# A searched instruction order replaced by another, with GpSimd as a second engine for two of VectorE's steps

## The chip, the cores and the metric

The kernel runs on one core of a Trainium2 chip. The core has five engines that work side by side, each with its own queue that is served strictly in order: TensorE (PE; weight loads and matmuls), VectorE (DVE), ScalarE (ACT; exponentials and tanh), GpSimd (POOL) and SyncE (SP), which here only issues DMA transfers. Engines wait for each other through semaphores. The metric is the device time of one execution in microseconds.

## The reference, cut to what matters

The input x has 2048 tokens of 640 channels in bfloat16. There are 32 heads of 20 channels, and the tokens are cut into 4 segments of 512. All weights are bfloat16.

```
h   = x + A(layernorm(x));   out = h + silu(layernorm(h) @ w1) @ w2        # w1: 640 x 1728

A:  q, k, v = x @ wq, x @ wk, x @ wv          # per head, per segment of 512 tokens
    for each segment:
        p     = softmax(q @ k.T * scale + causal mask)
        a_mem = (phi(q) @ M) / (phi(q) @ z + 1e-6)      # phi(t) = t + 1 if t > 0 else exp(t)
        o     = g * a_mem + (1 - g) * (p @ v)           # g = sigmoid(beta), per head
        M    += phi(k).T @ v ;  z += sum(phi(k))        # memory for the segments that follow
    return concat(o) @ wo
```

## The kernel before, in words

Work is declared as tasks, each with its engine (or the engines that may take it), what it reads and what it writes. In which order the tasks are issued, on which engine, and in which buffer slot, is written out by hand in one list, ORDER: an entry `qe030x/D:0` means task qe030x on VectorE with slot 0 of the pool that it allocates; /A is ScalarE, /G GpSimd, no letter the first engine that the task names. A tracker turns the list into one queue for each engine, with a semaphore wait wherever a task needs what another engine wrote. The list came from a search outside the kernel, over estimated durations; the kernel holds only its outcome. Nothing is reordered when it runs: a task that waits holds up all that stands behind it on its engine.

The tasks, by the first letters of their names:

- `x`, `w_`: loads of tokens and weights. `n1_st`, `n1_r`, `n1_ap`: statistics of the first layer norm (VectorE, L719 and L722), the power -0.5 of the variance (GpSimd, L735; its addition of eps on GpSimd, L732, or on VectorE, L729), the apply (VectorE, L741). `n2_` is the second layer norm, with the same lines.
- For segment 0 the normalized block of 128 tokens is transposed by TensorE (`n1_tp`, L750) and copied out of PSUM in one piece (`n1_te`, L759 on ScalarE, L760 on VectorE); for the others, and for n2, by a DMA transpose (`n1_tr`, `n2_tr`, L765).
- `pr`: q and k projections, five chunks each (L826); `qe` copies them out of PSUM (L834 ScalarE, L835 VectorE). In segment 0 each is done in two halves of two blocks, x and y. `v`, `ve`: the same for v (L793, L803, L804). The 12 columns of q and k that don't fit the first five chunks are gathered by small DMAs (`vt`) into a tile that is zeroed beforehand (`vz`, L847: one on VectorE, the one of segment 0 on GpSimd). In segment 0 q, k and the gathered tile lie in the memory of w2, which is loaded later.
- `re_wq`, `re_wk`: the weights of q and k put into chunk order by copies (L683 ScalarE, L685 VectorE).
- `qk`: scores of four heads at once (L912); `e`: their exponentials into a PT buffer of seven (ScalarE, L923); `mk`: the causal mask on the diagonal blocks (GpSimd, L934); `av`: the product with v (L955); `oe`: its evacuation (L968, L970); `tn`, `nm`, `ad`: turning back to tokens, division and adding (L984, L988; L1001 to L1021; GpSimd L1029).
- `ex`, `pha`, `phb`: phi(q) and phi(k), as the exponential (ScalarE, L866), max(t, 0) + 1 (VectorE, L873) and the minimum of the two (VectorE, L878). `kt`, `mz`, `ma`, `mb`: the memory, with a DMA transpose (L1072), products (L1077), sum and mask.
- `ot`, `wo`, `rs`: DMA transpose of the attention's output (L1116), output projection (L1124), residual (L1132). `h1`, `th`, `s`: first layer of the MLP (L1159, its short last tile L1153), tanh (L1168) and silu (L1174). `h2`, `o`, `out`: second layer (L1201), residual (L1214), store (L1219).
- `warm`: a tanh over a zero tile that fills the unused rows of w2 (L588), first on ScalarE. `fill`: matmuls on zeros, issued where TensorE has nothing to do (L607).

Segments overlap: projections of the next one, and the MLP of the one before, stand between the scores of this one.

Of the kernel before, what the change touches and what calls it, by code (L numbers as in the profile page):

```python
# [5 lines left out]
ACT = mybir.ActivationFunctionType  # L6
# [318 lines left out]
D = 640  # L325
# [31 lines left out]
qe000x:0 re_wk3 pr011x:1 qe020x:0 n1_tp2:2 x8:4,5,6,10 qe010x:0 n1_tp3:6 qe030x/D:0 re_wk4/A pr021x:4 qe011x n1_te2  # L357
qe001x/D pr041x:5 beta qe021x/D x4:7,8,9,11 n1_te3/D w_w1_0:0 n1_st9:1 w_w1_2 qk0x0:0 lsc0 qe041x:0 e0x0:0 e0x2
pr040x:4 pr031x:5 w_wv:0 n1_st7:3 pr041y:6 vz0/G:0 qk1x0:0 n1_r7 qe040x qe041y e1x2:1 lsc1 pr030y:7 pr040y:4 pr031y:6
qe031x/D e1x0 qe040y mk0x_0 w_w1_4 qe031y qk2x0:0 n1_st6:2 e2x2:2 qe030y/D pr011y:5 n1_st4:4 e2x0 pr001y:4 pr000y:7  # L360
n1_r4/D mk1x_0 qk3x0:0 mk2x_0 pr021y:6 qe000y/D qe021y/D vpad1 pr010y:7 n1_st5:6 qe001y/D mk2x_256 e3x2:3 e3x0 qe011y
n1_ap7:0 pr020y:2 vt04 vt08 v00:0 mk1x_256 qe020y vt01 qe010y ex011:0 ex031:1 vpad0 lsc2 qk4x0:2 ve00/D:0 vt011 e4x0:6
n1_r6/D pha011:0 vt05 n1_st8:5 v01:6 mk0x_256 vt02 e4x2 qk0yb0:0 vt06 mta0 ve01/D zf0 phb011 v03:4 pha001:1 mk3x_0
vt03 vt00 n1_r5/D lsc3 pha031:2 ex001:2 mtb0 e0yb0:4 e0yb2 n1_ap4:1 vt07 vt09 n1_ap6:2 av0x:6 av2x:7 n1_r9/D mk4x_0
vt010 n1_ap5:3 qk1yb0:0 ve03 mk3x_256 phb031 v02:4 e1yb2:5 oe0x/D:0 e1yb0 oe2x/D:1 mk4x_256 qk7x0:0 ve02/D e7x2:0 e7x0
n1_tr4:0 tn0x:6 mm1 mm6 n1_tr5 av1x:7 kt01:0 oe1x/D:0 n1_tr6 qk5x0:2 w_w1_3 tn1x:7 av3x:0 e5x0:2 nm0x:0,0 nm1x:1 e5x2
oe3x/D:0 mk7x_0 mk7x_256 tn2x:6 fill3:1 qk6x0:0 av4x:7 av7x:4 e6x2:1 nm2x:2 v11:5 pha051:0 e6x0 oe7x/D:1 phb001 ve11:1
mk0yb_0 n1_tr7 mk6x_0 mk6x_256 tn7x:3 v10:0 mk5x_0 ex051:0 ex021:1 oe4x/D:1 qk0ya0:4 mk5x_256 e0ya0:3 tn3x:2 mk0yb_256
zf1 nm7x:0 kt00:1 e0ya2 av6x:3 w_w2_4 ve10/D av5x:0 oe6x/D:0 nm3x:3 tn6x:1 oe5x/D:0 mk1yb_0 nm6x:1 fill2:3 qk1ya0:2
tn5x:0 tn4x:6 nm5x:2 av0y:7 pr100:1 e1ya2:1 nm4x:0 oe0y:1 e1ya0 w_wo:0 n1_st11:7 qk2yb0:4 ot1:0 mz00:0 mz01 phb051 ot0  # L370
mm7 mk1yb_256 e2yb0:6 ma00:0 v12:2 pha021:1 qe100/D:0 ve12/D e2yb2 qk2ya0:4 ex071:2 phb021 e2ya0:0 wo1:0 e2ya2
qk3ya0:2 rs1 n2_st1:0 e3ya0:2 mk2yb_0 wo0:6 n2_r1/D kt02:1 e3ya2 mk2yb_256 mm0 qk4ya0:0 rs0 e4ya0:3 kt03:0 n2_st0:4
v13:4 e4ya2 mz02:6 ve13/D av2y:7 qk3yb0:0 ex041:1 n2_r0 pha041:1 oe2y/D:0 mz03 pr141:4 e3yb2:4 n2_ap1:3 e3yb0 av1y:5
qk4yb0:0 phb041 ma01/A:1 n2_ap0:1 qe141/D:0 w_w1_1 tn0y:7 mk3yb_0 oe1y/D:1 ex061:0 kt05:1 nm0y:3 n2_tr1:0 e4yb2:6
e4yb0 n2_tr0 pr121:6 qk5ya0:2 tn2y:7 qe121/D:0 epsg1 nm2y:0 tn1y:0 e5ya2:0 pr101:1 e5ya0 qk5yb0:4 nm1y:1 pha141:2
# [901 lines left out]
```

## Time and profile before

| what | us |
|---|---|
| median of 3 runs (302.84 to 304.95) | 302.98 |
| the profiled execution | 302.65 |
| its span, first to last instruction | 300.9 |
| TensorE matmuls busy | 288.7 (96%) |
| VectorE busy | 234.4 (78%) |
| ScalarE busy | 230.5 (77%) |
| GpSimd busy | 135.8 (45%) |

The span is what the profile shows from the first instruction to the last; the execution's own time has 1.75 us around it. Matmuls are pipelined, so a busy TensorE isn't always one at its peak. In the views, "waits" give who waited for whom, in total, how often and the longest; the chain is followed back from the last instruction to what released it; a group's row has the line, the engine, the operation, its output and input, the count, then busy time, mean duration in ns, and idle time before it.

### The profile page before, as it was taken

The numbers are of one execution on the slowest core, as the hardware profiler recorded it, in microseconds if no ns is written. First come the engines' busy times: TensorE is split into PE (matmuls) and PEld (weight loads), VectorE is DVE, ScalarE is ACT, GpSimd is POOL, SyncE is SP. The second block draws the span as 40 slices with busy tenths as digits, with TensorE's granted clock in tenths as the row PEclk, the third lists the DMA queues.
The fourth block names the chain that finished last, engine by engine and source line by source line (L and its number), as shares of the span: only waits on it lengthen the run. The fifth ranks groups of instructions, "written<-read, shape, count | busy, mean of one in ns | idle before, by whom it ended". The sixth has DMA issues, their size and how long they took to land.

```text
span 300.9 us, 7531 instructions
## 1 busy us (share of the span) xinstructions
PE 288.7 (96%) x2994; PEld 169.5 (56%) x2994; DVE 234.4 (78%) x553; ACT 230.5 (77%) x337; POOL 135.8 (45%) x246
## 2 busy tenths in 40 slices
PE   8899888999999999989999899999999999999996
PEld 6675545555555455666643445556564457764575
DVE  6989887878798979879899976967868687835523
ACT  3889898999999999989889979998999741004500
POOL 2537843544566664445746715465395640200000
DMA  7953595556535320253662330233161004130002
GB/s 259 332 183 61 122 202 121 124 144 116 96 72 103 74 59 1 37 119 63 99 164 47 35 68 2 45 70 59 20 89 46 0 2 109 38 96 24 22 22 89
DMA packets 53603, 25.85 MB, mean 86 GB/s; under 512 B 44032, under 2 KB 52480, under 8 KB 53568
## 3 DMA queue, kind: packets, MB, share of 16 engines
q1 hardware_dynamic: 52144, 23.81, 36.5%
q10 hardware_dynamic: 1424, 1.56, 1.5%
q8 instruction: 24, 0.39, 0.6%
q14 instruction: 11, 0.09, 0.1%
HBM read 10.41 MB, written 2.62 MB: 43 GB/s over the span
## 4 chain that ended last, share of the span: by engine, by line
PE 66%; ACT 13%; DVE 12%; DMA 5%; issue 2%; POOL 1%
PE ps_all L1201 18%; PE ps_all L1159 15%; PE ps_all L826 10%; ACT PT L923 9%; PE ps_all L1124 7%; PE ps_all L912 6%; PE ps_all L955 5%; PE ps_all L793 3%; DMA oT<-otok 3%; DVE xn_rot L741 2%; DVE stt L719 2%; DVE oTs L970 1%; DMA xT<-xn_rot 1%; ACT th L1168 1%; ACT ex L866 1%
## 5 line engine op out<-in xcount | busy, mean ns | idle before, releaser
L923 ACT ACTIVATE PT<-ps_all 128x1024 bf16<-128x1024 f32 (+1 forms) x168 | 156.8, 987 | 10.0 <-PE ps_all L912 9.1
L934 POOL TENSOR_SCALAR_AFFINE_SELECT PT<-PT 128x512 bf16<-128x512 bf16 x128 | 80.8, 651 | 55.7 <-ACT PT L923 54.8
L1201 PE MATMUL ps_all<-w_sb,sT 128*128 128x320 bf16 (+2 forms) x462 | 65.5, 295 | 0.0
L1159 PE MATMUL ps_all<-hT,w_sb 128*128 128x512 bf16 (+1 forms) x325 | 63.3, 337 | 0.4 <-DVE otok L1003 0.2
L1168 ACT ACTIVATE th<-ps_all 128x512 f32<-128x512 f32 (+1 forms) x70 | 34.1, 509 | 34.6 <-PE ps_all L1159 27.0
L1201 PEld LDWEIGHTS ps_all<-w_sb,sT 128*128 128x128 bf16 x462 | 43.1, 98 | 19.0 <-issue 1.9
L1174 DVE SCALAR_TENSOR_TENSOR sT<-th,ps_all 128x512 bf16<-128x512 f32 (+2 forms) x70 | 38.0, 560 | 16.9 <-ACT th L1168 16.4
L1159 PEld LDWEIGHTS ps_all<-hT,w_sb 128*128 128x128 bf16 x325 | 29.3, 98 | 24.1 <-issue 3.2
L735 POOL TENSOR_TENSOR rst<-rst,eps_c 128x1 f32<-128x1 f32 x32 | 19.9, 623 | 23.7 <-DVE rst L729 22.3
L719 DVE BATCH_NORM_STATS2 stt<-x_tok 128x6 f32<-128x320 bf16 x64 | 27.9, 477 | 0.8 <-DMA x_tok<-in_A_x_dram 0.6
L1029 POOL TENSOR_TENSOR otok<-on 128x320 bf16<-128x320 bf16 x24 | 19.0, 797 | 17.8 <-DVE on L1021 17.8
L1124 PE MATMUL ps_all<-wo_sb,oT 128*128 128x320 bf16 x160 | 24.1, 300 | 1.9 <-DMA oT<-otok 1.6
L1214 DVE SCALAR_TENSOR_TENSOR x_tok<-ps_all,x_tok 128x640 bf16<-128x640 f32 (+3 forms) x18 | 13.3, 745 | 14.1 <-PE ps_all L1201 13.8
L955 PE MATMUL ps_all<-PT,Vx 128*32 128x256 bf16 (+3 forms) x576 | 23.7, 287 | 0.5 <-ACT PT L923 0.2
L970 DVE TENSOR_SCALAR oTs<-ps_all,lsc 128x512 bf16<-128x512 f32 (+1 forms) x33 | 20.3, 622 | 1.8 <-PE ps_all L955 1.1
L1021 DVE TENSOR_TENSOR on<-ps_all,rd 128x640 bf16<-128x640 f32 x24 | 19.8, 824 | 0.8
L1124 PEld LDWEIGHTS ps_all<-wo_sb,oT 128*128 128x128 bf16 x160 | 14.7, 98 | 9.7 <-issue 2.4
L741 DVE TENSOR_SCALAR xn_rot<-x_tok,mvt,rst 128x640 bf16<-128x640 bf16 x32 | 18.1, 572 | 2.2 <-POOL rst L735 2.1
L793 PE MATMUL ps_all<-wv_sb,xT 128*128 128x320 bf16 x120 | 18.2, 300 | 1.3 <-DMA xT<-xn_rot 1.0
L826 PE MATMUL ps_all<-xT,wqr 128*128 128x512 bf16 x75 | 18.7, 380 | 0.6 <-issue 0.6
L826 PE MATMUL ps_all<-xT,wkr 128*128 128x512 bf16 x75 | 18.7, 380 | 0.3 <-ACT PT L923 0.3
L1132 DVE TENSOR_TENSOR x_tok<-ps_all,x_tok 128x640 bf16<-128x640 f32 x16 | 13.1, 818 | 7.1 <-PE ps_all L1124 7.0
(90 smaller groups left out, 364.2 us busy)
## 6 DMA issues: line engine op xcount, KB each, us to landing
w_sb<-in_B_w_dram SPq DMA_DIRECT2D x5, 432.0 KB, 10.1
x_tok<-in_A_x_dram SPq DMA_DIRECT2D x3, 640.0 KB, 8.6
w_sb<-in_B_w_dram SPq DMA_DIRECT2D x3, 480.0 KB, 4.7
out_dram<-x_tok SPq DMA_DIRECT2D x9, 160.0 KB, 1.9
out_dram<-x_tok ACTq DMA_DIRECT2D x6, 160.0 KB, 1.8
QKV<-QK SPq DMA_DIRECT2D x12, 72.0 KB
sT<-in_A_wq_dram SPq DMA_DIRECT2D x1, 800.0 KB, 5.8
sT<-in_A_wk_dram SPq DMA_DIRECT2D x1, 800.0 KB, 7.4
```

The costliest lines, as they stand in the source:

```text
L719: T.add(DV, lambda e, hh=hh: e.bn_stats(out=stt[:, s, 6 * hh:6 * hh + 6], in_=xb[:, 320 * hh:320 * hh + 320]), reads=R((xa, xsub)), writes ...
L741: T.add(eng, lambda e: e.tensor_scalar(out=xn_rot[:, xn.slot, :], in0=x_tok[:, b % 12, :], scalar1=mvt[:, s, 0:1], scalar2=rst[:, s, :], o ...
L793: fns.append(lambda e, c=c, hh=hh: e.matmul(bank(ps, hh)[:, 0:320], lhsT=xT_[:, c, 128 * i:128 * i + 128], rhs=wv_sb[:, c, 320 * hh:320 * ...
L826: fns = [lambda e, kc=kc: e.matmul(bank(ps)[:, lo:hi], lhsT=wt[:, kc, c, :], rhs=xT_[:, kc, lo:hi], start=(kc == 0), stop=(kc == NC - 1)) ...
L923: T.add(AC, lambda e: e.activation(out=pt[:, pta.slot, q0:q0 + 2, 0:width], in_=sc3[:, b0:b0 + 2, 0:width], func=ACT.Exp, scale=SCALE), re ...
L934: T.add(PO, lambda e: e.affine_select(out=v, in_=v, pattern=[[0, 4], [1, 128]], compare_op=ALU.is_ge, fill=0.0, base=0, channel_multiplier ...
L955: fns.append(lambda e, j=j, r=r, h=h, pa=pa, pt=pt, co=co, q0=q0, ji=ji: e.matmul(bank(po)[32 * r:32 * r + 32, q0:hi], lhsT=Vx[:, vx.slot, ...
L1124: fns.append(lambda e, c=c, hh=hh: e.matmul(bank(ps, hh)[:, 0:320], lhsT=oT[:, c, 128 * i:128 * i + 128], rhs=wo_sb[:, c, 320 * hh:320 * h ...
L1159: fns = [lambda e, c=c: e.matmul(bank(ps)[:, lo:hi], lhsT=w1_sb[:, c, 128 * f:128 * f + 128], rhs=hT[:, c, lo:hi], start=(c == 0), stop=(c ...
L1168: T.add(AC, lambda e: e.activation(out=th[:, tha.slot, lo:hi], in_=bank(ps)[:, lo:hi], func=ACT.Tanh, scale=0.5), reads=R((ps, [0])), writ ...
L1174: T.add(DV, lambda e: e.scalar_tensor_tensor(out=sT[:, f, lo:hi], in0=th[:, tha.slot, lo:hi], scalar=1.0, in1=bank(ps)[:, lo:hi], op0=ALU. ...
L1201: fns.append(lambda e, f=f, t0=t0, fr=fr, hh=hh, n=n: e.matmul(bank(pa, hh)[:, 0:n], lhsT=sT[:, f, t0:t0 + 128], rhs=w2_sb[:, fr, c0 + 320 ...
```

## The change

The list ORDER is a new one, found by the same kind of search with all DMA transposes taken as late. Beside it some tasks change their form or get another engine to choose from:

- a max/add of phi (`pha`) and a norm apply (`ap`) may run on GpSimd; in the list 27 of 48 `pha` and 11 of 32 `ap` do (4 of the first norm, 7 of the second);
- the gathered tile is zeroed on VectorE only (`vz0` and `vz1`);
- q of segment 0 is projected and copied in three pieces, of block 0 (u), block 1 (v) and blocks 2 and 3 (y), where it was two halves;
- the evacuation of a segment-0 transpose is two instructions, of three and of two chunks, which may run on different engines; readers of it wait for both;
- there are eight PT buffers for seven.

The warm-up `warm` stands no longer first on ScalarE but among the exponentials of segment 0. TensorE's order keeps almost all of its sequence behind 90 us; the projections of segments 0 and 1 and the tail are reordered most. The core of the diff (of the list, its beginning):

```diff
-WH = [(0, 0), (0, 1), (1, 0), (1, 1)]
+WH = [(0, 0), (0, 2), (0, 1), (1, 0), (1, 2), (1, 1)]
+def XS(b0, b1):
+    return [10 * k + b for b in range(b0, b1) for k in range(2)]
...
 ORDER = """
-epsc:0 zpad x0:0 iota sel halfc x1:1 w_q:0 vz1:0 n1_st0:5 x2:2,3 n1_st1:3 n1_r0 n1_r1/D warm:0 n1_ap0:0 n1_ap1:1
-fill29:7 n1_tp0:0 n1_te0:0 re_wq2:0 re_wq3 n1_st2:7 fill3:2 n1_tp1:2 w_k n1_r2 n1_te1 n1_st3:0 re_wq0/A fill8:4
-pr020x:4 re_wq1/A re_wk0:0 pr030x:5 re_wq4 re_wk1/A mt0 n1_ap2:2 pr000x:6 re_wk2 pr010x:7 n1_r3 n1_ap3:3 pr001x:0
+iota:0 zpad x0:0 halfc vz0:0 sel epsc x1:1 n1_st1:0 n1_r1 w_q:0 n1_st0:1 n1_ap1:0 x2:2,3 n1_r0/D w_k beta re_wq1:0
+fill25:7 n1_tp1:0 n1_st3:2 n1_te1a:0 n1_ap0/G:1 fill11:2 n1_tp0:2 re_wq3 re_wq4 n1_r3 n1_te1b re_wq0/A pr010v:4
+n1_ap3/G:2 n1_te0b/D pr000v:6 pr030v:0 re_wq2/A n1_te0a qe000v:0 pr020v:5 pr040v:7 pr000u:1 qe010v:0 n1_st2:3
...
-        "PT": 7, "oTs": 2, "on": 2, "rd": 4, "otok": 1, "oT": 1,
+        "PT": 8, "oTs": 2, "on": 2, "rd": 4, "otok": 1, "oT": 1,
...
-        G.task(f"{tag}ap{b}", {DV: 0.46}, e_apply, ...)
+        G.task(f"{tag}ap{b}", {DV: 0.46, PO: 0.78}, e_apply, ...)
...
-                src = ps_all[:, 512 * ps.slot:512 * ps.slot + 640].rearrange("p (c t) -> p c t", c=NC)
-                o = dst[:, :, 128 * i:128 * i + 128]
+            for k, (c0, c1) in enumerate(((0, 3), (3, NC))):
+                    src = ps_all[:, 512 * ps.slot + 128 * c0:512 * ps.slot + 128 * c1].rearrange("p (c t) -> p c t", t=128)
+                    o = dst[:, c0:c1, 128 * i:128 * i + 128]
...
-                for hh, (b0, b1) in enumerate([(0, 2), (2, 4)] if s == 0 and (c, w) in SPLIT0 else [(0, 4)]):
+                for hh, (b0, b1) in enumerate(([(0, 1), (1, 2), (2, 4)] if w == 0 else [(0, 2), (2, 4)]) if s == 0 else [(0, 4)]):
...
-            G.task(f"vz{s}", {DV: 0.9, PO: 3.0}, lambda eng: T.add(eng, lambda e: e.memset(QKV_[:, :, :, :], 0.0),
+            G.task(f"vz{s}", {DV: 0.9}, lambda eng: T.add(eng, lambda e: e.memset(QKV_[:, :, :, :], 0.0),
...
-                G.task(f"pha{s}{c}{w}", {DV: 0.3}, e_phi, [src], [(pa, ["a"])], pr)
+                G.task(f"pha{s}{c}{w}", {DV: 0.3, PO: 0.64}, e_phi, [src], [(pa, ["a"])], pr)
```

The numbers at a task's engines are the search's own estimates; nothing in the running kernel uses them.

More of the change, by code (lines that the diff above doesn't have):

```diff
@@ L359 @@
[L359 to L363, printed above, removed]
@@ L827, in e_mm @@
                                                          start=(kc == 0), stop=(kc == NC - 1)) for kc in range(NC)]
-                        T.run(PE, fns, R((xTa, range(b0, b1)), (W[wk_], [c])), R((ps, [0])))
-                    G.task(f"pr{tag}", {PE: pe_c(*[n] * 5)}, e_mm, [(xTa, list(range(b0, b1))), (W[wk_], [c])],
+                        T.run(PE, fns, R((xTa, XS(b0, b1)), (W[wk_], [c])), R((ps, [0])))
+                    G.task(f"pr{tag}", {PE: pe_c(*[n] * 5)}, e_mm, [(xTa, XS(b0, b1)), (W[wk_], [c])],
                            [(ps, [0])], pr, mode="f", reserve=[qk[c]])
```

227 lines of the change are left out of this document (116 added, 111 removed).

## The prediction

> **What bounds the kernel now.** I read the stretches first, because two engines are both above 75% in the totals and only the stretches say which of them is full where. Per row: the stretch, its length, then busy time and instruction count of TensorE's matmuls (PE), its weight loads (PEld), VectorE (DVE), ScalarE (ACT) and GpSimd (POOL), the granted clock, and the DMA engines' share and GB/s.
>
> ```profile
> 0.00:16.00 16.00, 13.43 (x110) 10.42 (x111) 13.41 (x39) 8.98 (x21) 6.52 (x16) 1.00 0.85 302
> 16.00:60.00 44.00, 40.77 (x510) 24.28 (x508) 38.05 (x110) 40.59 (x63) 24.53 (x54) 1.00 0.63 129
> 60.00:120.00 60.00, 58.57 (x709) 32.32 (x708) 51.29 (x125) 59.51 (x85) 32.75 (x59) 1.00 0.40 85
> 120.00:200.00 80.00, 77.67 (x809) 43.28 (x807) 68.50 (x155) 73.42 (x106) 42.44 (x72) 1.00 0.35 65
> 200.00:241.00 41.00, 40.70 (x429) 22.67 (x430) 29.85 (x65) 36.06 (x46) 24.11 (x38) 1.00 0.27 49
> 241.00:301.00 60.00, 57.52 (x451) 36.54 (x439) 33.24 (x63) 11.96 (x22) 5.49 (x10) 1.00 0.19 50
> ```
>
> Five stages can be seen. Up to 16 us everything is being set up. From 16 to 60 ScalarE is busy 40.59 of 44 us, from 60 to 120 it is full (59.51 of 60): its exponentials set the pace. From 120 to 200 no one is quite full: TensorE 77.67 and ScalarE 73.42 of 80. From 200 on TensorE is full, and what ends there is a fixed amount of matmul work: a microsecond won before 200 is a microsecond off the end, and one won after it, off TensorE's path, is nothing. VectorE, with 86% (38.05 of 44; 51.29 of 60; 68.50 of 80) from 16 to 200, is close behind the two; GpSimd is at 55%. The granted clock is 1.00 throughout, so it plays no part.
>
> Next the waits, in total, times and longest, and then the chain that ended last, in order of time (start, length, what):
>
> ```profile
> PEld ps_all L912 <- ACT PT L923: 11.9, 37, 0.7
> ACT PT L923 <- PE ps_all L912: 9.1, 21, 0.7
> PEld ps_all L1124 <- DMA oT<-otok: 2.1, 2, 1.1
> PEld ps_all L793 <- DMA xT<-xn_rot: 1.2, 1, 1.2
> PEld ps_all L955 <- POOL PT L934: 0.5, 2, 0.3
> ```
>
> ```profile
> 41.56 4.43 DMA oT<-otok
> ...
> 120.14 0.55 PE ps_all L1159 x5
> ...
> 128.65 3.67 DMA oT<-otok
> ...
> 169.15 4.05 DMA xT<-xn_rot
> ...
> 282.02 1.09 PE ps_all L1201 x8
> ...
> 284.21 14.35 PE ps_all L1201 x118
> ```
>
> TensorE's scores (L912) wait for ScalarE's exponentials (L923) 37 times and the other way round 21 times: the two are in lockstep. Three DMA transposes are on the chain, but TensorE stands idle for them only 2.1 + 1.2 = 3.3 us. For a mask of GpSimd the value product (L955) waits 0.5 us in all.
>
> **The change part by part.** First the start. This is its timeline (start, length, engine):
>
> ```profile
> 3.04 1.27 ACT L588 ACTIVATE w_sb<-zpad 128x1280 bf16<-128x1280 bf16 x1
> 10.91 2.87 POOL L847 MEMSET w_sb<- 128x3072 bf16 x1
> 10.94 2.90 DVE L685 COPY wkr<-sT 128x400 bf16<-128x400 bf16 x2
> 11.32 2.68 DVE L741 TENSOR_SCALAR xn_rot<-x_tok,mvt,rst 128x640 bf16<-128x640 bf16 x1
> 14.06 0.28 PEld L750 LDWEIGHTS ps_all<-ident,xn_rot 128*128 128x128 bf16 x5 [1.62 <-DVE xn_rot L741]
> 15.94 0.81 ACT L923 ACTIVATE PT<-ps_all 128x768 bf16<-128x768 f32 x1
> ```
>
> *The zeroing of the gathered tile* (task vz0) is the 2.87 us GpSimd memset. While it runs, two copies of VectorE and a norm apply stand still: the apply shows 2.68 us, ends with the memset, and TensorE waits 1.62 us for it. The usual price of the apply is the median of the first row below.
>
> ```profile
> L741 DVE TENSOR_SCALAR xn_rot<-x_tok,mvt,rst x32: 395/441/2682, 5.9 to 264.6; 128x640 bf16<-128x640 bf16 x32
> L873 DVE TENSOR_SCALAR phiK<-QKV x6: 278/480/722, 99.9 to 179.1; 128x512 bf16<-128x512 bf16 x6
> L847 DVE MEMSET QKV<- x1: 1338/1338/1338, 1.7 to 1.7; 128x1536 uint32 x1
> ```
>
> So 2.68 - 0.44 = 2.2 us of VectorE's stall goes. On VectorE the memset costs 1.34 us (the other tile's, L847) in a place at the head of the list that the other tile's memset held; that one now runs near 45 us and takes 1.34 us of VectorE there, beside exponentials. What is late next is ScalarE: of its 8.98 busy us before 16 some 2.55 (the table load and the 1.27 us warm-up of the first row) are over by 4.3, so from the first transposed block near 7.5 it works 6.4 of 8.4 us, and can let the first exponential come at most 2.0 us sooner. The split evacuations and the q of segment 0 in pieces of one block let work begin after one block, but make more, smaller ScalarE instructions in front of that exponential (18 in its list, 13 before, the warm-up left out of both). Bounds 0 and -2.0; I take **-1.1 us**, the middle, as nothing in the trace is nearer to either end.
>
> *Moved off VectorE:* 27 of 48 max/add (L873) and 11 of 32 norm applies (L741). On VectorE they cost what the groups say (last rows' columns: busy us, mean ns); on GpSimd this trace shows neither. The nearest rows are its mask and its add:
>
> ```profile
> L741 DVE TENSOR_SCALAR xn_rot<-x_tok,mvt,rst 128x640 bf16<-128x640 bf16 x32 | 18.1, 572 | 2.2 <-POOL rst L735 2.1
> L934 POOL TENSOR_SCALAR_AFFINE_SELECT PT<-PT 128x512 bf16<-128x512 bf16 x128 | 80.8, 651 | 55.7 <-ACT PT L923 54.8
> L1029 POOL TENSOR_TENSOR otok<-on 128x320 bf16<-128x320 bf16 x24 | 19.0, 797 | 17.8 <-DVE on L1021 17.8
> ```
>
> One input of 512 columns takes 651 ns, two inputs of 320 take 797. Both moved operations read one tensor, so I take the mask's rate: 0.65 us for a max/add, 0.81 for an apply; the upper bound is the add's rate, 797/320 ns a column: 1.28 and 1.59. GpSimd gains 27 x 0.65 + 11 x 0.81 = 26.5 us (upper bound 52) and loses the 2.87; between 16 and 241 it goes from 55% to some 65%. VectorE loses 27 x 0.28 to 0.48 and 11 x 0.57, about 16 us in all. That is no time by itself: VectorE sets the pace nowhere for long. It counts where TensorE and ScalarE wait for it.
>
> The Trainium skill speaks against such a move. "SBUF — State Buffer", section "Who interferes with whom", says that VectorE in its two-port modes and GpSimd lock each other out for a whole instruction, and "Perfetto Trace Analysis", section "Optimizing Scalar/DVE Operations", that offloading between them therefore might not help. By that rule (the trace agrees in the apply that lasted as long as the memset, and in max/adds of 278 and 722 ns for one shape) part of the 16 us comes back as longer VectorE instructions; it is the third rival below.
>
> *Loads* change their place in SyncE's queue: the value and output weights come before those of the MLP, and three of the five pieces of its first layer are issued behind the first output projections, where one was.
>
> ```profile
> w_sb<-in_B_w_dram SPq DMA_DIRECT2D x2, 432.0 KB, 4.1
> ```
>
> Such a piece lands 4.1 us after its issue between 30 and 80 us. The last output projection of that pair lies more than 7 us of listed matmuls ahead of the first MLP group, so I cost them at nothing; without that cover it is up to 4 us, once.
>
> *ScalarE's work by stage.* Comparing the lists up to the same exponential, ScalarE does more before 60 us (up to the exponentials of e6ya): the warm-up (1.27), one ex (0.64), one memory evacuation (0.32), one more output evacuation (0.47), the q and k pieces equal in number. Sum +2.7 us.
>
> ```profile
> L866 ACT ACTIVATE ex<-QK 128x512 bf16<-128x512 bf16 x25 | 15.8, 640 | 0.0
> L1088 ACT ACTIVATE Mz<-ps_all 128x168 f32<-128x168 f32 x1 | 0.3, 317 | 0.0
> L968 ACT ACTIVATE oTs<-ps_all,lsc 128x256 bf16<-128x256 f32 x1 | 0.5, 469 | 0.0
> L968 ACT ACTIVATE oTs<-ps_all,lsc 128x512 bf16<-128x512 f32 x6 | 4.0, 695 | 1.3 <-PE ps_all L955 1.3
> ```
>
> Against it stand 44 - 40.59 = 3.4 us in which ScalarE idles there now. VectorE sheds 2 to 4 us in this stage and an eighth score buffer (PT) lets more exponentials run ahead; I take half the idle time, -1.7, so the stage comes to **+1.0** (bounds -0.7 and +2.7). From 60 to 120 ScalarE is the clock, and its list is shorter by the ex moved ahead (0.64) and an output evacuation moved out (0.695), the q and k pieces equal: **-1.3**. From 120 to 200 it gets two output evacuations and gives back smaller pieces: +0.8 of work against 80 - 73.42 = 6.6 us of idle time, which covers it. There the list puts two more groups of first-layer matmuls (0.55 us each in the chain) ahead of the output projection that waited for the 3.67 us transpose, and as many as before ahead of the v of segment 3 that waited 1.2 us; both waits together are at most 2.1. With the freed VectorE I take **-0.7** (bounds -3.3, half of the idle time, and +0.8).
>
> *From 200 to the end* the matmuls are the same and TensorE is dense: **0**. The four last norm applies go to GpSimd, into one queue with its powers.
>
> ```profile
> L1132 DVE TENSOR_TENSOR x_tok<-ps_all,x_tok 128x640 bf16<-128x640 f32 x16 | 13.1, 818 | 7.1 <-PE ps_all L1124 7.0
> L719 DVE BATCH_NORM_STATS2 stt<-x_tok 128x6 f32<-128x320 bf16 x64 | 27.9, 477 | 0.8 <-DMA x_tok<-in_A_x_dram 0.6
> L735 POOL TENSOR_TENSOR rst<-rst,eps_c 128x1 f32<-128x1 f32 x32 | 19.9, 623 | 23.7 <-DVE rst L729 22.3
> hT<-xn_rot SPq DMA_TRANSPOSE x16, 2.6
> ```
>
> After the last output projection 78 matmuls of the second layer stand ahead of the first layer of segment 3's MLP, at 1.09 us for eight 10.6 us. The chain behind that projection (residual 0.8, statistics twice two halves 1.9, power 0.6, two applies 1.6, transpose 2.6) needs 7.5, so it is covered, unless an apply costs the upper bound on all four: 3.1 us more, and TensorE stands still where it did not. The ten output stores now issued from ScalarE's queue (seven before) fall mostly in its empty tail.
>
> Sum: -1.1 + 1.0 - 1.3 - 0.7 = **-2.1 us** on the profiled execution, whose 300.9 us span took 302.65 us as a whole. The median shown, 302.98, is 0.33 above it, so I forecast 300.9 us.
>
> **The rivals.** *VectorE was the hidden cause.* If the idle time of ScalarE from 16 to 60 goes nearly whole (-3.4 in place of -1.7) and half of that from 120 to 200 (-3.3 for -0.7), the sum is -6.4 and the time 296.6. For it: VectorE is at 86% over those stretches and in front of many evacuations. Against it: the wait rows name ScalarE and TensorE for each other, seldom VectorE.
>
> *GpSimd becomes late (slower).* Its queue is served in order, and 27 max/adds and 5 applies now stand among the masks of 16 to 241 us. Behind a mask wait the value product (L955), and behind that TensorE's whole queue. Decides: a mask that ends after TensorE has come to its value product; today that costs 0.5 us. If one in three of the 32 passes its 0.7 us on, that is 7.5 us: 308.4. The add's rate in place of the mask's would double it.
>
> *The relief is not felt.* If the lock returns VectorE's stalls, or ScalarE is simply the clock from the first exponential on, then only work counts: -1.1 + 2.7 - 1.3 + 0.4 = +0.7, or 303.7 us.
>
> **How the numbers follow.** Forecast 0.38, hidden cause 0.24, late GpSimd 0.24, no relief 0.14. A measurement of this kernel tells about 1%, 3 us, from no change. Below 299.95 lie nearly all of the second case and a quarter of the first (own range 299 to 303): 0.32. Above 306.0 lies most of the third: 0.22. Within: 0.46. The range from 296.8 to 307.5 leaves out the lower half of the hidden cause's spread and the upper half of the late GpSimd's, some 0.2.
>
> **What would show it.** First exponential near 14.8 us and no GpSimd memset of 3072 columns; the apply at L741's place never above 1 us before 16; ScalarE busier than 41 us of its first 44 after the first exponential; VectorE near 219 us, GpSimd near 159; max/adds on GpSimd at 0.65 us; the wait of L955 for POOL still near 1 us. I am wrong if that wait is several us, if a max/add on GpSimd costs over 1 us, or if TensorE shows gaps after 200 us.

## The result and the profile after

The changed kernel takes **324.39 us** (median; 323.95 to 324.71) where the kernel before took 303.97 beside it: a ratio of 1.0672, with a 95% interval of 1.0618 to 1.0725. The forecast was 300.9 us, with a range up to 307.5: the kernel takes 23.5 us more than forecast, and the profiled span, which was to fall by 2.1 us, grew from 300.9 to 322.2 us. In the changed file these lines have moved by 4 or 5: the max/add is L878 (L873 before), the minimum L883, the norm apply L745 (L741), the mask L939 (L934), the value product L960 (L955), the exponential L928 (L923), the first MLP layer L1164 (L1159).

The page of the changed kernel: its span, the busy time of each engine, the granted clock in 40 slices (9 is full speed), and the chain that ended last.

```profile
span 322.2 us, 7569 instructions
...
PE 291.6 (91%) x2989; PEld 170.5 (53%) x3015; DVE 227.0 (70%) x516; ACT 232.0 (72%) x343; POOL 211.8 (66%) x286
...
PEclk9999979999999999599999999999999999999999
...
PE 41%; POOL 27%; DVE 16%; DMA 5%; ACT 5%; issue 3%; SPq 1%; POOLq 1%; DVEq 0%; ACTq 0%
```

GpSimd's 135.8 us became 211.8, where 159 were forecast, and GpSimd now makes up 27% of the chain (1% before). VectorE fell only to 227.0 (forecast 219). TensorE's clock, at full speed before, has two dips.

The stretches, with the columns as in the prediction (PE, PEld, DVE, ACT, POOL, clock):

```profile
0.00:16.00 16.00, 11.86 (x124) 9.49 (x124) 10.71 (x39) 7.88 (x23) 9.26 (x19) 1.00 0.83 288
16.00:60.00 44.00, 39.08 (x477) 22.84 (x475) 35.28 (x90) 39.57 (x62) 36.84 (x56) 0.96 0.49 117
60.00:120.00 60.00, 54.57 (x664) 31.87 (x662) 47.29 (x116) 56.04 (x78) 41.66 (x64) 1.00 0.46 97
120.00:200.00 80.00, 72.14 (x700) 38.81 (x706) 58.96 (x130) 66.17 (x98) 65.91 (x77) 0.94 0.32 60
```

ScalarE was full from 60 to 120 us; now it idles there for 4 us, and between 120 and 200 for 13.8 of 80. TensorE and ScalarE both wait more, and GpSimd, busy 84% of the time from 16 to 60 us and 82% from 120 to 200, is full where they wait. That is what the waits say (who waits for whom: total us, times, longest):

```profile
ACT PT L928 <- PE ps_all L917: 18.1, 24, 4.8
POOL phiK L878 <- DMA phiKt<-phiK: 7.3, 3, 3.8
DVE phiK L883 <- POOL phiK L878: 6.9, 2, 5.3
PE ps_all L960 <- POOL PT L939: 6.8, 7, 3.8
PE ps_all L1164 <- DMA hT<-xn_rot: 3.7, 2, 2.8
DVE phiQ L883 <- POOL phiQ L878: 3.0, 4, 2.2
PEld ps_all L754 <- POOL xn_rot L745: 2.8, 2, 2.1
```

The value product's wait for a mask, 0.5 us before, is 6.8. VectorE waits 9.9 us (6.9 and 3.0) for max/adds that GpSimd now has, a wait that did not exist. The reason stands in GpSimd's groups (busy us, mean ns of one):

```profile
L745 POOL TENSOR_SCALAR xn_rot<-x_tok,mvt,rst 128x640 bf16<-128x640 bf16 x11 | 27.8, 2533 | 0.8
L878 POOL TENSOR_SCALAR phiQ<-QK 128x512 bf16<-128x512 bf16 x8 | 15.4, 1933 | 0.0
L939 POOL TENSOR_SCALAR_AFFINE_SELECT PT<-PT 128x512 bf16<-128x512 bf16 x128 | 81.6, 655 | 21.1 <-ACT PT L928 20.0
```

A max/add takes about 1.93 us on GpSimd (1.92 to 2.04 by group) and an apply 2.53, where 0.65 and 0.81 were forecast and 1.28 and 1.59 were its upper bounds. The mask beside them costs what it did. All 27 max/adds come to 52.4 us, all 38 instructions to 80.2, against 26.5 in the forecast.

### The profile page after: what moved, and what is told of

Same layout as the page of the kernel before. It is cut to its first block, busy times and chain, and to the rows that moved or that the text cites. A ratio compares the mean times of both kernels' runs of the same rounds, so it can differ in the third digit from the quotient of the medians.

```text
span 322.2 us, 7569 instructions
## 1 busy us (share of the span) xinstructions
PE 291.6 (91%) x2989; PEld 170.5 (53%) x3015; DVE 227.0 (70%) x516; ACT 232.0 (72%) x343; POOL 211.8 (66%) x286
## 3 DMA queue, kind: packets, MB, share of 16 engines
q10 hardware_dynamic: 1856, 1.93, 1.7%
## 4 chain that ended last, share of the span: by engine, by line
PE 41%; POOL 27%; DVE 16%; DMA 5%; ACT 5%; issue 3%; SPq 1%; POOLq 1%; DVEq 0%; ACTq 0%
PE ps_all L1164 11%; PE ps_all L1206 10%; POOL xn_rot L745 7%; PE ps_all L831 7%; POOL PT L939 6%; POOL phiQ L878 5%; ACT PT L928 4%; POOL rst L739 4%; POOL phiK L878 4%; PE ps_all L917 4%; PE ps_all L1129 3%; PE ps_all L960 3%; DVE stt L723 2%; DMA hT<-xn_rot 2%; PE ps_all L798 2%
## 5 line engine op out<-in xcount | busy, mean ns | idle before, releaser
L928 ACT ACTIVATE PT<-ps_all 128x1024 bf16<-128x1024 f32 (+1 forms) x168 | 156.3, 983 | 19.1 <-PE ps_all L917 18.1
L939 POOL TENSOR_SCALAR_AFFINE_SELECT PT<-PT 128x512 bf16<-128x512 bf16 x128 | 81.6, 655 | 21.1 <-ACT PT L928 20.0
L1164 PE MATMUL ps_all<-hT,w_sb 128*128 128x512 bf16 (+1 forms) x314 | 60.8, 339 | 4.8 <-DMA hT<-xn_rot 3.7
L1173 ACT ACTIVATE th<-ps_all 128x512 f32<-128x512 f32 (+2 forms) x70 | 33.6, 505 | 40.1 <-PE ps_all L1164 33.7
L1179 DVE SCALAR_TENSOR_TENSOR sT<-th,ps_all 128x512 bf16<-128x512 f32 (+1 forms) x70 | 37.8, 557 | 18.3 <-ACT th L1173 17.5
L1164 PEld LDWEIGHTS ps_all<-hT,w_sb 128*128 128x128 bf16 x325 | 30.0, 99 | 28.0 <-DMA hT<-xn_rot 4.1
L960 PE MATMUL ps_all<-PT,Vx 128*32 128x256 bf16 (+3 forms) x576 | 24.2, 296 | 8.3 <-POOL PT L939 6.8
L739 POOL TENSOR_TENSOR rst<-rst,eps_c 128x1 f32<-128x1 f32 x32 | 18.1, 569 | 16.2 <-DVE rst L733 14.7
L745 POOL TENSOR_SCALAR xn_rot<-x_tok,mvt,rst 128x640 bf16<-128x640 bf16 x11 | 27.8, 2533 | 0.8
L960 PEld LDWEIGHTS ps_all<-PT,Vx 128*32 128x32 bf16 x576 | 12.9, 99 | 18.5 <-issue 8.3
L745 DVE TENSOR_SCALAR xn_rot<-x_tok,mvt,rst 128x640 bf16<-128x640 bf16 x21 | 12.3, 589 | 9.5 <-POOL rst L739 9.5
L831 PE MATMUL ps_all<-xT,wkr 128*128 128x512 bf16 x69 | 17.5, 379 | 1.3 <-ACT PT L928 0.6
```

The lines of the kernel that those rows point to most:

```text
L739: T.add(PO, lambda e: e.tensor_tensor(out=rst[:, s, :], in0=rst[:, s, :], in1=eps_c[:, 1:2], op=ALU.pow), reads=R((st, ["r"]), (C, ["half" ...
L745: T.add(eng, lambda e: e.tensor_scalar(out=xn_rot[:, xn.slot, :], in0=x_tok[:, b % 12, :], scalar1=mvt[:, s, 0:1], scalar2=rst[:, s, :], o ...
L831: fns = [lambda e, kc=kc: e.matmul(bank(ps)[:, lo:hi], lhsT=wt[:, kc, c, :], rhs=xT_[:, kc, lo:hi], start=(kc == 0), stop=(kc == NC - 1)) ...
L928: T.add(AC, lambda e: e.activation(out=pt[:, pta.slot, q0:q0 + 2, 0:width], in_=sc3[:, b0:b0 + 2, 0:width], func=ACT.Exp, scale=SCALE), re ...
L939: T.add(PO, lambda e: e.affine_select(out=v, in_=v, pattern=[[0, 4], [1, 128]], compare_op=ALU.is_ge, fill=0.0, base=0, channel_multiplier ...
L960: fns.append(lambda e, j=j, r=r, h=h, pa=pa, pt=pt, co=co, q0=q0, ji=ji: e.matmul(bank(po)[32 * r:32 * r + 32, q0:hi], lhsT=Vx[:, vx.slot, ...
```

## The experiments

Two theories stood at first. **Price**: the new order is about as good as the old one, and the durations of the 38 instructions on GpSimd, with what queues behind them, are the loss. **Order**: the new list is itself worse. The edits below are shown shortened.

### The moves undone, together and apart

```diff
-... n1_ap0/G:1 ...  pha001/G:0 ...
+... n1_ap0:1   ...  pha001:0   ...      # e1: all 38; e2: the 11 applies; e3: the 27 max/adds
```

> The changed kernel with all 27 max/adds and 11 norm applies back on VectorE, at the same places of the list. Theory P (the price on GpSimd, 1.93 and 2.53 us an instruction, is the whole loss): 300 to 304 us, and GpSimd busy near 132 us. Theory O (the new order itself, with its pieces and its moved warm-up, is worse): still 312 us or more, with TensorE waiting for other things than GpSimd.

> The changed kernel with only the 11 applies back on VectorE; the 27 max/adds stay on GpSimd (27 x 1.93 = 52 of the 80 us that the 38 take there). P, if the loss goes with GpSimd's time: 303 + 20 x 52/80 = 316 us. If instead the applies are what is waited for (they stand ahead of transposes that TensorE needs), 308 or less. O: 316 or more.

> The changed kernel with only the 27 max/adds back on VectorE; the 11 applies stay on GpSimd (28 of 80 us). P, if the loss goes with GpSimd's time: 303 + 20 x 28/80 = 310 us. If the max/adds in front of the masks are what counts: 305. If the applies are: 316.

| run | median us | ratio to before, 95% interval |
|---|---|---|
| e1, all on VectorE | 305.14 | 1.0077 [1.0041, 1.0113] |
| e2, only the max/adds on GpSimd | 314.01 | 1.0349 [1.0284, 1.0415] |
| e3, only the applies on GpSimd | 313.12 | 1.0350 [1.0279, 1.0420] |
| changed kernel, both on GpSimd | 324.39 | 1.0672 [1.0618, 1.0725] |

The order alone costs 0.8%. From there 27 max/adds add 0.027 to the ratio, 11 applies another 0.027, both 0.060: nearly a sum, 18 us of the 20. Order as the main cause has fallen. GpSimd's busy time alone is not the measure either: the applies take 28 of the 80 us there, which would be 7 of the 20 us lost (e3 at 310 us) against 13 for the max/adds (e2 at 316), and each half lost about 8.

### Where it is lost

The first exponential of several groups of scores was matched in all traces. Its start in e1 is in the second column; the others show how much later it starts than in e1 (us):

```
exponential   e1       changed  e2     e3     e7     e8     e9
e0x0          15.83    +0.9     -0.2   +0.8   +0.9   +0.8    0.0
e6ya0         60.93    +4.2     +0.8   +1.0   +2.1   +2.4   -1.3
e15a0        116.89    +4.7     +1.1   +1.1   +4.0   +2.9   -2.8
e16a0        124.53   +12.6     +9.0   +1.1   +4.0  +10.6   -2.8
e26a0        202.64   +15.0     +9.5   +1.9   +6.4  +13.0   -3.5
e31a0        240.53   +17.2     +9.9   +3.6   +8.6  +15.2   -3.5
span         302.3    +19.9     +9.9   +7.9  +12.9  +15.2   -3.5
```

Two of the losses lie at one place each: 7.9 us between e15a0 and e16a0, only where these max/adds are on GpSimd, and 2.7 us behind e31a0 (4.3 in e3, 4.4 in e7), only where the last applies are. This is the changed kernel around the first place (start, length, engine; in brackets the idle time before, and who ended it), and then the stretches 125 to 129 and 129 to 137 us:

```profile
119.59 3.81 POOL L878 TENSOR_SCALAR phiQ<-QKV 128x512 bf16<-128x512 bf16 x2
...
123.35 3.81 POOL L878 TENSOR_SCALAR phiQ<-QK 128x512 bf16<-128x512 bf16 x2
...
127.11 1.81 POOL L939 TENSOR_SCALAR_AFFINE_SELECT PT<-PT 128x512 bf16<-128x512 bf16 x3
...
129.07 2.33 PE L960 MATMUL ps_all<-PT,Vx 128*32 128x512 bf16 x32 [3.80 <-POOL PT L939]
```

```profile
125.00:129.00 4.00, 0.27 (x2) 0.00 (x0) 0.51 (x2) 2.23 (x4) 4.00 (x6) 0.85 0.00 0
129.00:137.00 8.00, 7.08 (x62) 3.32 (x63) 4.42 (x8) 2.32 (x3) 7.93 (x8) 0.50 0.36 74
```

Four max/adds in one row, 7.54 us, stand ahead of the masks; TensorE stands still for 3.80 us, and behind that its clock is granted at 0.50 for 8 us. In stretches of 1 us the clock is 0.88 from 127 to 128, 0.50 from 128 to 138 and 1.00 after that. The wait is thus paid a second time, by an estimate from the 7.9 us less the 3.80 as some 4 us of half speed. The Trainium skill, "TensorE: Matmul & The Clock Gate", section "What's actually happening", says that TensorE falls to half clock when about 3.4 us have passed idle. The traces agree in the half clock and not in the time: here it fell some 2.5 us after the last matmul (which ends at 125.27), and of three waits of 2.7 us in the tail, below, two brought it and one did not. The other dip has no such wait:

```profile
40.00:48.00 8.00, 7.00 (x86) 3.25 (x83) 6.11 (x15) 6.79 (x10) 8.00 (x8) 0.79 0.64 130
```

TensorE is busy for 7 of these 8 us, with short instructions and short waits, and e7 and e8 have the dip too, e2 and e3 not; what brings it is left open.

```diff
-pha160/G:0 pha170/G:0 ... pha220/G:0 pha210/G:0
+pha160:0   pha170:0   ... pha220:0   pha210:0        # e7
-n2_ap14/G:1 ... n2_ap13/G:2 ... n2_ap15/G:0 ... n2_ap12/G:3
+n2_ap14:1   ... n2_ap13:2   ... n2_ap15:0   ... n2_ap12:3   # e8
```

> The changed kernel with four of its 27 max/adds back on VectorE, those of pha160, pha170, pha220 and pha210, which stand in one row ahead of the masks at 119.6 to 127.2 us. Theory 'place': a GpSimd instruction costs where a mask stands behind it that TensorE waits for, and these four carry the 7.4 us that the kernel loses between the exponentials e15a0 and e16a0; 316.5 to 318.5 us. Theory 'load': the loss is spread over the 38 by GpSimd's total, and four of them are worth 4/38 of 19 us, 2.0 us; 322 to 323 us.

> The changed kernel with the last four norm applies (n2_ap12 to n2_ap15) back on VectorE. If the cover of the tail fails as the trace shows it (TensorE stands 2.75 us for the transposed tile behind them), the time falls by 2.5 to 3.1 us, to 321.3 to 321.9 us, as 4 x (2.53 - 0.44) = 8.4 us of the chain go and some cover is left over. If the transposes themselves are what comes late, nothing changes: 324 us.

With the four back, e7 takes 316.98 us, a ratio of 1.0456 [1.0409, 1.0503]: 0.0216 less than the changed kernel, 6.5 us for four instructions. The step in the table is gone (4.0 and 4.0), and so is the half clock at this place. The value product in e7, and the stretch around it:

```profile
124.41 1.27 PE L960 MATMUL ps_all<-PT,Vx 128*32 128x512 bf16 x32
```

```profile
119.00:127.00 8.00, 7.01 (x86) 3.33 (x88) 7.29 (x16) 6.62 (x9) 6.22 (x6) 1.00 0.15 28
```

The same 32 matmuls take 1.27 us in place of 2.33, with no wait. **Place** decides, then, not GpSimd's total, by which the four were worth 2.0 us.

The tail of the changed kernel, and of e8 with its four applies on VectorE:

```profile
276.30 10.76 PE L1206 MATMUL ps_all<-w_sb,sT 128*128 128x320 bf16 x78
289.82 9.66 PE L1164 MATMUL ps_all<-hT,w_sb 128*128 128x512 bf16 x44 [2.75 <-DMA hT<-xn_rot]
```

```profile
275.74 9.26 PE L1206 MATMUL ps_all<-w_sb,sT 128*128 128x320 bf16 x67
285.06 9.66 PE L1164 MATMUL ps_all<-hT,w_sb 128*128 128x512 bf16 x44
```

e8 takes 319.35 us, 1.0545 [1.0495, 1.0595]. That is 3.8 us less by the ratios, where 2.5 to 3.1 were expected and each interval reaches 1.5 us to either side; its trace shows the 2.7 us behind e31a0 gone and the second layer running into the first without a gap. (Up to e6ya0 e7 and e8 issue the same as the changed kernel and are about 2 us earlier in their profiled runs, so that much differs from one execution to the next.)

The same wait can cost more. In e7, whose tail is that of the changed kernel, the same 44 matmuls take 11.35 us in place of 9.66, and the clock is at half behind the wait (in e3 likewise: a wait of 2.71, then 11.35 us):

```profile
281.11 11.35 PE L1164 MATMUL ps_all<-hT,w_sb 128*128 128x512 bf16 x44 [2.74 <-DMA hT<-xn_rot]
```

```profile
281.00:285.00 4.00, 3.89 (x11) 1.41 (x11) 0.00 (x0) 0.00 (x0) 0.00 (x0) 0.57 0.00 0
```

In all traces of this case the time from one change of the clock to the next is a whole number of steps of 3.41 us, and a dip lasts one, two or three of them. That it depends on where a wait falls in such a step whether it costs clock too would fit these three tails; it was not tried.

### What sets the price on GpSimd

```diff
-tensor_scalar(out=o, in0=iv, scalar1=0.0, scalar2=1.0, op0=max, op1=add)
+tensor_scalar(out=o, in0=iv, scalar1=0.0, scalar2=None, op0=max)              # e5: one of these
+tensor_copy(out=o, in_=iv)
+tensor_tensor(out=o, in0=iv, in1=iv, op=add)
+tensor_scalar(out=o, in0=iv, scalar1=0.5, scalar2=1.0, op0=mult, op1=add)
+tensor_scalar(... op0=add, op1=max) / (add alone) / (mult alone) / (subtract, mult)   # e10
-tensor_scalar(out=xn, in0=x, scalar1=mean, scalar2=rstd, op0=subtract, op1=mult)
+tensor_scalar(... mean, rstd, op0=mult, op1=add) / (0.5, 1.0, subtract, mult) / (mean, mult alone)   # e10
```

> The changed kernel with its 27 max/adds on GpSimd given five forms: as they are (5), maximum alone without the addition (6), a plain copy (6), the tensor added to itself (5), a multiplication and an addition (5); phi is therefore not computed in 22 of them. Theory 'by operation': GpSimd pays for each of the two arithmetic steps, so the two-step forms take 1.92 us, the one-step form and the sum of two tensors about 1.0 to 1.3 us, the copy about 0.65 us, the mask's duration. Theory 'by column': every form of 512 columns takes 1.9 us whatever it computes, and only the mask is cheaper. My forecast's rate (one input read, 0.65 us) would have to show in the copy at least.

> The changed kernel with its GpSimd instructions in further forms, so phi and the norm are not computed in most of them. Max/adds: as they are, addition before maximum, one addition, one multiplication, subtraction before multiplication. Applies: as they are, multiplication and addition by columns, subtraction and multiplication by constants, one multiplication by a column. Theory 'maximum': the maximum is the dear step, 1.9 us in either order, and all forms without it take 0.62 us. Theory 'known pairs': multiply-then-add has a way of its own and everything else takes 1.4 to 1.9 us. For the apply: if the columns in place of constants make it dear, the form with constants takes 0.76 us and the other column forms over 1.5; if the subtraction does, multiplication and addition by columns takes about 0.8 us.

Each form had its own line; most of these forms leave phi or the norm out, and the runs are read for their rows alone (they took 314.25 and 317.29 us, once each). Rows of e5 (count, then shortest, median and longest ns): the maximum alone, the copy, the sum of two tensors, multiplication and addition, and the maximum and addition as they are:

```profile
L881 POOL TENSOR_SCALAR phiQ<-QK x2: 1483/1486/1490, 83.7 to 131.1; 128x512 bf16<-128x512 bf16 x2
L884 POOL COPY phiQ<-QK x2: 609/610/610, 118.7 to 138.9; 128x512 bf16<-128x512 bf16 x2
L886 POOL TENSOR_TENSOR phiK<-QK x2: 1203/1210/1216, 123.8 to 148.8; 128x512 bf16<-128x512 bf16 x2
L889 POOL TENSOR_SCALAR phiK<-QKV x1: 618/618/618, 162.2 to 162.2; 128x512 bf16<-128x512 bf16 x1
L892 POOL TENSOR_SCALAR phiQ<-QKV x2: 1923/1925/1927, 115.4 to 232.8; 128x512 bf16<-128x512 bf16 x2
```

Rows of e10: the apply as multiplication and addition by columns, with constants, and as it is; then addition and maximum, one addition, one multiplication, subtraction and multiplication:

```profile
L749 POOL TENSOR_SCALAR xn_rot<-x_tok,mvt,rst x3: 874/875/875, 10.7 to 269.5; 128x640 bf16<-128x640 bf16 x3
L753 POOL TENSOR_SCALAR xn_rot<-x_tok x3: 2353/2359/2366, 53.0 to 272.1; 128x640 bf16<-128x640 bf16 x3
L760 POOL TENSOR_SCALAR xn_rot<-x_tok,mvt,rst x3: 2503/2512/2562, 7.3 to 275.9; 128x640 bf16<-128x640 bf16 x3
L895 POOL TENSOR_SCALAR phiQ<-QKV x1: 1928/1928/1928, 118.5 to 118.5; 128x512 bf16<-128x512 bf16 x1
L898 POOL TENSOR_SCALAR phiK<-QKV x1: 1489/1489/1489, 108.9 to 108.9; 128x512 bf16<-128x512 bf16 x1
L901 POOL TENSOR_SCALAR phiK<-QKV x1: 1492/1492/1492, 125.7 to 125.7; 128x512 bf16<-128x512 bf16 x1
L904 POOL TENSOR_SCALAR phiK<-QKV x1: 1930/1930/1930, 168.7 to 168.7; 128x512 bf16<-128x512 bf16 x1
```

Both theories of the first run fall, and "maximum" of the second. It is not the columns (0.61 to 1.93 us for the same 512), not the number of steps (two steps cost 0.62, one costs 1.49), not the maximum (addition alone costs as much) and not the scalar columns (2.36 us without them). **Known pairs** stands: multiply-then-add is as cheap as a copy for 512 columns (for the apply's 640, by columns, it takes 0.88 us, and the copy of e9 0.72), and every other form with a constant that was tried takes 1.5 us with one step and 1.9 with two. The forecast's rate, one tensor read in some 0.65 us, is real for the mask that it was taken from, for the copy and for this pair, and for none of the other forms tried. The Trainium skill, "GPSIMD Engine Reference", section "4.1 Engine selection", holds one-input elementwise work to run at about line rate there; the trace agrees for the copy (0.61 us) and the multiply-add, and not for the max/add (1.93), where the measurement decides.

### The forecast at its own price

```diff
+if eng == PO:   # on GpSimd: 27 max/adds as mult+add (0.62 us), 11 applies as copies (0.72 us)
```

> The changed kernel, all 38 instructions on GpSimd, but in forms that cost there what the forecast took: the 27 max/adds as a multiplication and an addition (0.62 us in the forms run), the 11 norm applies as plain copies (0.76 us, estimated from the copy's 0.61 us for 512 columns); phi and the norm are therefore not computed there. If only the price failed, this gives the forecast's 300.9 us, within its own range of 299 to 303. If the relief of VectorE buys nothing, it gives the 305 us of the new order with all 38 on VectorE. If GpSimd is late even at this price, as the rival had it, 308 us.

It takes **300.53 us**, 0.9933 [0.9908, 0.9959]; the forecast was 300.9. Order, engines and dependences are those of the changed kernel; only the form of 38 instructions differs, and with it their duration (this kernel leaves phi and the norm out in them), and the 22 to 24 us, by ratios and by medians, are gone. Its waits hold no value product behind a mask any more; what is left of GpSimd's lateness is 0.4 us of one weight load (L997) behind a mask, and

```profile
DVE phiQ L891 <- POOL phiQ L883: 0.8, 1, 0.8
DVE phiK L891 <- POOL phiK L883: 0.8, 1, 0.8
```

and in its tail the first layer follows the second without a gap:

```profile
257.74 8.59 PE L1214 MATMUL ps_all<-w_sb,sT 128*128 128x320 bf16 x62
266.16 9.01 PE L1172 MATMUL ps_all<-hT,w_sb 128*128 128x512 bf16 x41
```

Against e1 (305.14) it also shows that the relief of VectorE is worth 4.6 us, if GpSimd does the work cheaply.

### The start, the warm-up, and copies for GpSimd

```diff
-epsc:0 zpad ... vz1:0 n1_st0:5 ... pr041y:6 vz0/G:0 qk1x0:0 ... qk3ya0:2 rs1
+epsc:0 zpad ... vz0:0 n1_st0:5 ... pr041y:6 qk1x0:0 ... qk3ya0:2 vz1:0 rs1    # e4, from the kernel before
-re_wk4/A
+re_wk4/G                                                                       # e12, on top of e4
-... mk6x_256 warm:0 oe7x/D:0 ...
+warm:0 fill25:7 ...                                                            # e11, on top of e1
```

> The kernel before with one thing changed: the gathered tile of segment 0 is zeroed on VectorE at the head of its list, where the other tile's zeroing stood, and that one is moved to near 47 us on VectorE. No 2.87 us memset on GpSimd, no 2.68 us apply. As predicted: the first exponential 1.1 us sooner and 302 us. Rival: ScalarE is late next and nothing is won, 303.

> The new order with all 38 instructions on VectorE (305.1 us, 1.0077 of before) and the warm-up tanh back at the head of ScalarE's list. If the 1.27 us of warm-up among segment 0's exponentials are what the new order loses on ScalarE, as the forecast's term for 16 to 60 us has it, 303.9 us and a ratio of 1.003 to 1.005. If ScalarE's idle time swallowed it, nothing changes: 1.007 to 1.008.

> The kernel before with the gathered tile zeroed on VectorE (300.4 us, 0.9905 of before), and with one group of three weight copies (re_wk4, 0.94 us on ScalarE ahead of the first exponential) on GpSimd, whose queue the removed memset has left free. A copy is a cheap form there (0.61 us for 512 columns, so about 0.48 for 400, 1.4 for the three). If what GpSimd can do cheaply is worth giving to it where ScalarE sets the pace, 0.5 to 0.9 us less: 299.6 to 299.9, ratio 0.987 to 0.989. If its copies hold up VectorE as the memset did, no gain or a loss of up to 1 us: 300.4 to 301.4.

e4, the old order with the gathered tile zeroed on VectorE and nothing else of the change, takes **300.41 us**, 0.9905 [0.9874, 0.9936]: it beats both kernels, and the 302 us that the forecast's 1.1 would have given. (The first exponential's gain stays at 1.65 us up to e16a0 and has become 3.1 by e24a0; what adds the second part is not settled.) Its timeline at the places of the apply that lasted 2.68 us and of the first exponential, which started at 15.94:

```profile
11.64 0.45 DVE L741 TENSOR_SCALAR xn_rot<-x_tok,mvt,rst 128x640 bf16<-128x640 bf16 x1
...
14.28 1.51 ACT L923 ACTIVATE PT<-ps_all 128x768 bf16<-128x768 f32 x2
```

The apply takes its usual time, and the first exponential comes 1.66 us sooner.

e11 takes 305.04 us, 1.0081 [1.0050, 1.0113], the same as e1: the moved warm-up costs nothing that can be measured, which fits idle time of ScalarE that swallows it. e12 takes 300.41 us, 0.9920 [0.9895, 0.9946]: the first exponential comes 0.24 us earlier than in e4, and the end does not move measurably, where 0.5 to 0.9 us were hoped for.

### Cheap forms with nothing left out

phi(t) is also max(t + 1, min(exp t, 1)), and t + 1 can be written t x 1 + 1; the apply is x r + (-m r):

```diff
+tensor_scalar(out=o, in0=iv, scalar1=1.0, scalar2=1.0, op0=mult, op1=add)              # GpSimd, for max/add
+scalar_tensor_tensor(out=o, in0=ex, scalar=1.0, in1=o, op0=min, op1=max)               # VectorE, for the minimum
+tensor_scalar(out=mean, in0=mean, scalar1=rstd, scalar2=-1.0, op0=mult, op1=mult)      # GpSimd, 128 x 1
+tensor_scalar(out=xn, in0=x, scalar1=rstd, scalar2=mean, op0=mult, op1=add)            # GpSimd, the apply
```

e14 puts them into the new order, e13 into the old one, in which e6 has the 38 instructions in their dear form; e15 is e4 with the 27 of phi.

> The kernel before with its old order, and in it the same 27 max/adds and 11 norm applies on GpSimd. Theory 'price': the durations on GpSimd are the loss, in any order; they cost 17 to 19 us here as they did in the new order (8.9 and 8.0 apart, 19.3 together), so 320 to 323 us. Theory 'order': the new order puts these instructions where they hurt, the old one, in which they stand where VectorE had them, would lose much less (under 10 us, below 314) or, not being made for it, much more (over 330).

> The kernel before in its old order with the same 38 instructions on GpSimd that cost it 36 us, now in the form that is cheap there, and nothing left out: t x 1 + 1 on GpSimd (0.62 us) and max(t + 1, min(exp t, 1)) on VectorE, which is the same phi; the apply as x r + (-m r) (0.88 us, behind one small instruction for -m r). If the 36 us were the price of the instructions, they go wholly: 299 to 303 us, as VectorE is also relieved. If the old order is unfit for GpSimd's taking them at any price, over 310 us remain.

> The changed kernel in its new order, with the same cheap forms and nothing left out. The run with cheap forms that left phi and the norm out took 300.5 us; here each apply has a small instruction more (0.2 to 0.6 us) and the 27 minimums of VectorE become an instruction with two steps (0.1 us more each, 3 us of VectorE in all, beside other work). If the choice of form is the whole cause, 300.5 to 303 us; if the left-out arithmetic hid something else, nearer to 324 us.

> The kernel before with the gathered tile zeroed on VectorE (300.4 us) and the 27 max/adds on GpSimd in the cheap form, the applies left on VectorE. The cheap forms took 4.5 us off the new order (305.1 to 300.5 us) by relieving VectorE; if the old order gains half of that, 298 us, ratio 0.98 to 0.987. If VectorE holds nothing up there, 300.4 us, and if the two-step instruction that takes the minimum's place delays it, 301 to 302.

| run | median us | ratio to before, 95% interval |
|---|---|---|
| e6, old order, dear forms | 338.80 | 1.1186 [1.1120, 1.1252] |
| e13, old order, cheap forms | 310.67 | 1.0259 [1.0203, 1.0316] |
| changed kernel: new order, dear forms | 324.39 | 1.0672 [1.0618, 1.0725] |
| e14, new order, cheap forms | 302.74 | 0.9994 [0.9968, 1.0020] |
| e15, e4 with 27 cheap max/adds | 304.41 | 1.0048 [1.0019, 1.0076] |

e14 came out as expected: the whole computation, in the new order, with only the form changed, loses nothing. The other three missed. e6 lost 36 us, not 17 to 19, so the price depends on the order, and the new list, made for these instructions on GpSimd, halves it (with its smaller pieces and its eighth PT buffer; their parts were not tried alone). The cheap forms take 28 of the 36 back, and 8 stay. e15 is 4 us slower than e4, not faster. One part of that is seen in its groups, where the two-step instruction (L893) stands beside the minimum that it replaces (L896):

```profile
L893 DVE SCALAR_TENSOR_TENSOR phiQ<-ex,phiQ 128x512 bf16<-128x512 bf16 x13 | 10.5, 814 | 0.0
...
L896 DVE TENSOR_TENSOR phiQ<-phiQ,ex 128x512 bf16<-128x512 bf16 x11 | 5.7, 517 | 0.3 <-ACT ex L876 0.3
```

It takes 0.30 us more, not 0.1: what GpSimd takes off VectorE (0.3 us a max/add) comes back. VectorE's total is 236.1 us, 233.5 in e4. A part lies in the clock. Its mean in the profiled runs is 0.950 in e6, 0.989 in e13 and 0.994 in e15 (at 0.50 from 34 to 37 us), and 1.000 in e4 and e14. If every microsecond of half speed cost half a microsecond, that would be an estimated 17 of e6's 36 us, 3.4 of e13's 8 and 1.8 of e15's 4; that is the most it can have been. What else holds up e13 and e15 is not settled.

## Why the prediction was wrong

**The step that failed is the price**: "Both moved operations read one tensor, so I take the mask's rate: 0.65 us for a max/add, 0.81 for an apply; the upper bound is the add's rate". Measured: 1.93 and 2.53, three times the value and half as much again as the bound. The bound was not one: it took the number of inputs for what sets a GpSimd duration, and e5 and e10 show that with one input and the same columns it is the arithmetic. With 0.62 and 0.72 us in place of the dear forms (e9) the same list gives 300.5 us. The forecast said that it would be wrong if a max/add cost over 1 us, and it was.

**The late GpSimd** was the right rival with the wrong size. Its place (a mask behind GpSimd's new work, then the value product, then TensorE's queue) is what e7 shows. Its own formula, one in three of 32 passing its duration on, gives with the measured durations (27 x 1.94 + 5 x 2.53) / 3 = 21.7 us, 322.6 in all. That this comes near is luck: the loss is not spread evenly as it supposed, four instructions carry a third of it, about half of that, by the estimate above, as lost clock. That the granted clock "plays no part" was true of the trace before, and not of what a new 3.8 us wait does to it: the changed kernel's mean is 0.979 over 322 us, at most 6.8 us of its 20, and the forecast had this term at nothing.

**The start**, -1.1 us. The mechanism was right: e4 shows -1.66 at the first exponential from the memset alone, inside the bounds 0 and -2.0. In the new list it is not there: +0.83 in the changed kernel, and still only -0.1 with everything on VectorE (e1) and -0.15 at the forecast's price (e9). The changed kernel's own part is two applies of the first norm, which the forecast had at 0.81 us on GpSimd and placed nowhere on the path:

```profile
7.29 2.70 POOL L745 TENSOR_SCALAR xn_rot<-x_tok,mvt,rst 128x640 bf16<-128x640 bf16 x1
...
10.04 0.45 PE L754 MATMUL ps_all<-ident,xn_rot 128*128 128x128 bf16 x5 [1.84 <-POOL xn_rot L745]
...
10.99 0.49 ACT L764 ACTIVATE hT<-ps_all 128x384 bf16<-128x384 f32 x1 [1.62 <-DVE hT L765]
```

The last row points to the rest: the two halves of one evacuation, on two engines, do not run beside each other, and one waits for the other (0.87 us in e1 and 1.02 in e9 at the same place). That this is what takes back the 1.5 us between e4 and e9 was not tried alone.

**ScalarE by stage**, cumulated in e9 against before: at e6ya0 -0.9 (forecast -0.1), at e16a0 -0.5 (-1.4), at e24a0 -2.1 (-2.1), at the end of the span -2.1 (-2.1). The sum is right by luck: the start gave 0.15 in place of 1.1, the stage to 60 us won 0.8 where 1.0 was to be lost, the next lost 0.4 where 1.3 was to be won, and between e24a0 and the end the difference runs from -3.1 (e26a0) to -0.1 (e31a0), as the lists differ in order there. The +1.27 of the warm-up was none (e11).

**The tail**: "covered, unless an apply costs the upper bound on all four: 3.1 us more". By the forecast's own sums, 7.5 + 3.1 against 10.6 us of cover, even the bound would just have been covered. The applies cost more than the bound (4 x (2.53 - 0.81) = 6.9 us over the forecast, 3.8 beyond the cover), and 2.75 us came; covered in e9, gone in e8.

**The relief not felt**, as a rival, has fallen: e9 gains 4.6 us over e1. But the relief is smaller than the 16 us forecast: VectorE's busy time is 234.7 us in e1, 224.2 in e9 and 227.0 in the changed kernel. The forecast took the applies at a mean of 0.57 us that the one of 2.68 us had raised (median 0.44). And the 24 minimums of phi(q), which stayed on VectorE, take 11.9 us in e1, 12.9 in e9 and 14.3 in the changed kernel, so that a part does come back as longer instructions; what lengthens them was not tried.

## What to carry to other kernels

A duration on another engine is read from the same instruction there, arithmetic and all, or measured with one short run before anything is moved; a neighbour with the same shape is no bound. Before giving an in-order engine longer work, look for what stands right behind it that a full engine waits for: four max/adds in one row cost more (7.9 us in the traces, 6.5 by the medians) than the other 23 together (2.0 in e2), and the 3.8 us wait behind them was paid twice, since the clock fell. If the work must go there, look for an equal expression in the engine's cheap form, and count what the other half of the expression then costs where it stays.

## What the runs showed that was not expected

On GpSimd, 128 x 512 in bfloat16: a copy 0.61 us, multiply-then-add 0.62, one multiplication 1.49, one addition 1.49, maximum alone 1.49, maximum and addition 1.93 in either order, subtract-then-multiply 1.93. Doing both steps of the right pair takes less than half the time of either step alone. And TensorE's clock: 3.80 us without work brought some 10 us at half speed; of three waits of 2.7 us, two brought 3.4 us of it (e3, e7) and one none (the changed kernel).
